# Windowed attention followed by a mixture of adapters: v cast by GpSimd's DMA queue and turned in one piece, q kept in natural order, and four smaller edits

## The chip, the cores and the metric

The kernel runs on one core of a Trainium2 chip. The metric is the device time of one execution in microseconds (us); three executions of the kernel before gave 203.4, 205.75 and 207.98 us, so the median is 205.75 us. The engines are called TensorE (PE in the profile, PEld for its weight loads), VectorE (DVE), ScalarE (ACT), GpSimd (POOL) and SyncE (SP, which only issues DMAs here).

## What is computed

```python
def _attn_ref(q, k, v):            # each (8, 8, 576, 64) float32
    scores = scale * np.matmul(q, k.transpose(0, 1, 3, 2))
    mask = np.abs(pos[:, None] - pos[None, :]) <= 32
    scores = np.where(mask, scores, -1000000000.0)
    ...
    return np.matmul(attn, v)

def _moe_ref(x, w_gate, A, B):     # x (4608, 512): the attention's output, heads side by side
    logits = x @ w_gate            # 8 experts, the best 2 are kept, softmax over these
    ...
            delta[mask] += w[mask, k, None] * (x[mask] @ A[e] @ B[e])
    return x + delta
```

There are 64 pairs of batch and head, each with 576 rows of 64. A row attends only to rows at most 32 away, so the scores are made in blocks: 64 keys against the 128 queries around them.

## The kernel before

**Tiles.** The 64 pairs are taken two at a time: one half of the partitions (64 of them) holds a pair of the first four batches, the other half one of the last four (`g` in the code). So there are 32 units of 9 blocks of 64 rows. The rows of all units, 32 x 576, are cut into 9 load tiles of 2,048 rows; the tiles are numbered t = 0 to 8. A tile's q and k are 1 MB of float32 each, and so is its v.

**q and k** (`load_qk`, L326 to L383). SyncE loads a tile with partitions of 16 rows each (`run_view`, L313); tile 0 comes in two pieces of 64 partitions. Two casts to float16 per tensor and tile (L350) run on GpSimd (for tile 0 partly on VectorE and ScalarE). TensorE turns each cast piece by eight matmuls with the identity (L359), and ScalarE or VectorE evicts the result from PSUM (L368) into `qT`, or into `kc` for k. GpSimd then spreads `kc` into `kT` (L379), a tile whose off-diagonal quarters were zeroed at the start, so that one 128-row weight holds both halves' keys. In `qT` and `kc` the 16 rows of a partition lie 128 columns apart.

**v** (`load_v`, L385 to L408). SyncE issues four DMAs of 32 partitions each per tile (L392; 2 KB runs in `half_view`), GpSimd casts the tile in one instruction (L397), and VectorE turns it straight into `vt` by two stream transposes of 32x32 blocks, one for each 64 partitions (L406). `vraw` has two buffers and `v16` one.

**Scores** (`score`, 36 groups of 8 blocks). Two matmuls put the mask into PSUM (L460), then each block's matmul adds the scores (L465); its queries are read from `qT` with 16 rows apart and its output is written to PSUM in the same strided order (`p[:, i].rearrange("m (p r) -> m r p", r=16)`). ScalarE's exp evicts a group into `PT` (L472).

**The rest.** `pv` multiplies by v (L500), and VectorE normalises (L510, L523) into `xs`. `moe` runs once for each quarter s of the units (for the last quarter in three parts): turn x (L550), evict (L560), logits and A (L587), gating by some twelve small VectorE instructions (L598 to L634), turn z (L643, L650), multiply by B (L663). VectorE then adds x while it evicts (L678) into one of four `ob` buffers, and SyncE stores from there (L688).

**What sets the order.** Every piece is an `Op` with the engines that may do it, a duration, the buffers that it holds and a due number (`prio`). `Plan.order` puts all pieces in one list by these estimates before anything runs, choosing an engine and a buffer for each; each engine then runs its share strictly in that order. A piece that holds a buffer waits until those who held it before are done; SyncE's DMA issues stand in the same kind of order, loads and stores in one queue. PSUM has three 1,024-column float32 tiles (`W`) for scores, PV, logits and adapter output, and two float16 tiles (`T`) for transposes.

Of the kernel before, what the change touches and what calls it, by code (L numbers as in the profile page):

```python
# [45 lines left out]
class Op:  # L46
    def __init__(self, eng, fn, bufs, need, make, prio, dma):
        self.eng, self.fn = eng, fn
        self.bufs, self.need, self.make = bufs, need, make
        self.prio, self.dma = prio, dma  # L50
        self.takes = len(eng) > 1 or fn.__code__.co_varnames[:1] == ("eng",)
        self.on = self.start = self.end = self.ready = None


class Plan:
    COST = {"DVE": 0.6}
# [25 lines left out]
    def order(self, slack):  # L82
# [23 lines left out]
        while left:  # L106
            can = []
            low = 1e9
            for o in left:
# [14 lines left out]
                for e, dur in o.eng.items():  # L124
# [3 lines left out]
                    ends.append((t + dur + self.COST.get(e, 0.0), t, e))  # L128
# [35 lines left out]
def kernel(  # L164
# [14 lines left out]
    POOLS = {"W": 3, "T": 2, "raw": 4, "vraw": 2, "c16": 5, "v16": 1,  # L179
# [5 lines left out]
    def many(name, shape, dt, pool=sb):  # L185
# [90 lines left out]
    for i, t in enumerate(phys["PT"]):
        fh = P.first_hold("PT", i)
        zeros(t[:, :, 0:64], fh, -90 + 5 * i)
        zeros(t[:, :, 192:256], fh, -90 + 5 * i)
    for i, t in enumerate(phys["vt"]):  # L280
        fh = P.first_hold("vt", i)
        zeros(t[0:64, :, D:], fh, -88 + 30 * i)
        zeros(t[64:128, :, 0:VD2], fh, -88 + 30 * i)
# [5 lines left out]
        op("DVE", 0.3, ones, bufs=[fh], need=[f"vz{i}"], prio=-88 + 30 * i)  # L289
# [33 lines left out]
    def load_qk(w, t):  # L323
        pieces = [(0, 64), (64, 64)] if t == 0 else [(0, 128)]
        raw = buf("raw", f"raw{w}{t}")
        src = run_view(w)  # L326
        dst = buf({"q": "qT", "k": "kc"}[w], f"{w}T{t}")
        if w == "q":
            qT[t] = dst
        else:  # L330
            kT[t] = buf("kT", f"kT{t}")
        due = 32 * t
        lp = -80 + due + (0 if w == "q" else 1)
        for pi, (p0, pn) in enumerate(pieces):
            op("SP", 0.4, lambda p0=p0, pn=pn: nc.sync.dma_start(  # L335
                out=ap(raw)[p0:p0 + pn], in_=src[128 * t + p0:128 * t + p0 + pn]),
                bufs=[raw], make=[(w, t, p0, "raw")], prio=lp + 0.5 * pi, dma=DMA_MB * pn / 128)
            for hf in range(2):
# [4 lines left out]

                def cast(eng=eng, p0=p0, pn=pn, hf=hf, c16=c16):
                    o = ap(c16)[p0:p0 + pn].rearrange("p r (g d) -> p r g d", g=2)
                    i = ap(raw)[p0:p0 + pn].rearrange("p g (f r d) -> p f r g d", f=2, d=D)[:, hf]
# [4 lines left out]
                dur = {"POOL": pool, "ACT": act, "DVE": dve32}[eng](1024)  # L351
                op(eng, dur, cast, bufs=[raw, c16], need=[(w, t, p0, "raw")],
                   make=[(w, t, p0, hf, "16")], prio=due - 30 + (0 if w == "q" else 1) + 0.1 * hf + .5 * pi)
                tp = buf("T", f"tp{w}{t}_{p0}_{hf}")

# [385 lines left out]
```

## Time and profile before

| | |
|---|---|
| median of 3 runs | 205.75 us |
| the profiled execution's own time | 205.5 us |
| its span, first to last instruction | 203.6 us |
| mean granted TensorE clock | 0.914 of 2.4 GHz |
| read from and written to memory | 28.85 MB and 9.44 MB |

The profile is one execution. Busy times of engines overlap; a group of instructions has the line, the engine, the operation, output<-input, and shapes as partitions x elements. "Idle before, <-releaser" is the time for which the engine waited just before the group and what ended the wait. DMA issues are listed under SP (SPq), the engine whose queue they stand in, and are not counted as busy.

### The profile page before, as it was taken

Reading aid. Unit: us, or ns where it says so; the run is one execution under the profiler, and the core shown is the slowest. Engines: PE = TensorE matmul, PEld = TensorE weight load, DVE = VectorE, ACT = ScalarE, POOL = GpSimd, SP = SyncE. Lnnn points to the kernel's source line nnn. Section 1 sums busy time; section 2 is a strip of 40 time slices with the busy share of each in tenths; the row PEclk is TensorE's granted clock in tenths of the full one; section 3 lists DMA queues with packets and bytes.
Section 4 is the critical chain, followed back from the end, with each engine's and each line's share of the span. In section 5 each row is a group of like instructions: output and inputs, shape, how many; then the busy total and the mean of one; then the engine's idle time right before and its main releaser. Section 6 shows DMA issues by size and latency. Waiting matters only on the chain.

```text
span 203.6 us, 3782 instructions
## 1 busy us (share of the span) xinstructions
PE 137.2 (67%) x1512; PEld 112.6 (55%) x1512; DVE 136.1 (67%) x230; ACT 92.5 (45%) x110; POOL 76.9 (38%) x80
## 2 busy tenths in 40 slices
PE   0250797949798919729329997659799958777450
PEld 0140586848697918418218897547589944665200
DVE  4641609729778797734046799978798487869652
ACT  8990149533586506700702864508447425143300
POOL 5345882568486458078233654720400000000000
PEclk9999999999999966985966999979999999999955
DMA  5999999999999999999559980001920002912252
GB/s 130 222 216 342 288 340 226 268 373 196 301 248 239 291 226 274 220 284 256 189 182 307 367 174 0 3 0 36 337 94 0 3 2 72 335 60 84 99 206 77
DMA packets 16705, 38.53 MB, mean 189 GB/s; under 512 B 2736, under 2 KB 2736, under 8 KB 16688
## 3 DMA queue, kind: packets, MB, share of 16 engines
q1 hardware_dynamic: 16688, 38.30, 67.5%
q8 instruction: 12, 0.20, 0.4%
q14 instruction: 5, 0.04, 0.1%
HBM read 28.85 MB, written 9.44 MB: 188 GB/s over the span
## 4 chain that ended last, share of the span: by engine, by line
DMA 45%; PE 27%; DVE 15%; issue 3%; POOL 3%; ACT 2%; SPq 2%; DVEq 0%; POOLq 0%; ACTq 0%
DMA vraw<-in_v_dram 28%; DMA raw<-in_k_dram 11%; PE W L465 8%; DMA out_dram<-ob 6%; DVE ob L678 5%; PE W L500 5%; PE W L460 4%; PE T L550 3%; PE W L587 3%; PE W L663 3%; DVE xs L523 2%; DVE vt L406 2%; DVE zs L634 2%; PE T L643 1%; SPq L335 1%
## 5 line engine op out<-in xcount | busy, mean ns | idle before, releaser
L472 ACT ACTIVATE PT<-W 128x1024 f16<-128x1024 f32 x36 | 36.8, 1024 | 65.0 <-PE W L465 59.2
L465 PEld LDWEIGHTS <-kT 128*128 128x128 f16 x304 | 35.2, 135 | 28.9 <-issue 20.6
L350 POOL CAST c<-raw 128x1024 f16<-128x1024 f32 (+1 forms) x37 | 37.6, 1038 | 31.6 <-DMA raw<-in_q_dram 18.0
L465 PE MATMUL W<-qT,kT 128*128 128x128 f16 (+3 forms) x304 | 47.5, 319 | 0.9 <-POOL kT L379 0.9
L359 PE MATMUL T<-ident,c 128*128 128x128 f16 (+1 forms) x320 | 23.7, 227 | 31.6 <-POOL c L350 20.7
L406 DVE STREAM_TRANSPOSE vt<-v 64x1024 f32<-64x1024 f32 x18 | 37.6, 2088 | 9.9 <-POOL v L397 9.7
L460 PE MATMUL W<-mask,perm 128*128 128x512 f16 x72 | 32.7, 454 | 15.5 <-DVE ob L678 7.5
L359 PEld LDWEIGHTS <-c 128*128 128x128 f16 (+1 forms) x320 | 19.9, 106 | 35.2 <-POOL c L350 21.7
L500 PE MATMUL W<-vt,PT 128*128 128x130 f16 x416 | 31.2, 228 | 3.3 <-ACT PT L472 1.7
L678 DVE TENSOR_TENSOR ob<-W,xs 128x1024 f32<-128x1024 f32 (+1 forms) x23 | 23.9, 1078 | 14.0 <-DMA out_dram<-ob 9.1
L500 PEld LDWEIGHTS <-PT 128*128 128x128 f16 x416 | 27.7, 103 | 6.4 <-issue 5.2
L523 DVE TENSOR_TENSOR xs<-W,rc 128x640 f16<-128x640 f32 (+1 forms) x34 | 26.7, 785 | 1.4 <-PE T L550 0.2
L379 POOL COPY kT<-kc 64x1024 f32<-64x1024 f32 (+1 forms) x20 | 19.8, 990 | 19.0 <-ACT kc L368 17.9
L397 POOL CAST v<-vraw 128x2048 f16<-128x2048 f32 x9 | 17.0, 1894 | 17.3 <-DVE vt L406 6.7
L368 ACT COPY kc<-T 128x1024 f16<-128x1024 f16 (+1 forms) x16 | 14.3, 908 | 11.2 <-POOL kT L379 6.0
L368 ACT COPY qT<-T 128x1024 f16<-128x1024 f16 (+1 forms) x14 | 13.6, 979 | 10.1 <-PE T L359 9.1
L510 DVE RECIPROCAL rc<-W 128x10 f32<-128x10 f32 (+1 forms) x34 | 7.1, 210 | 14.4 <-PE W L500 14.2
L663 PE MATMUL W<-Bw,zT 128*128 128x512 f16 x40 | 13.4, 417 | 3.4 <-ACT zT L650 1.4
L560 ACT COPY xT<-T 128x1024 f16<-128x1024 f16 x12 | 11.9, 1010 | 4.9 <-PE T L550 4.8
L550 PE MATMUL T<-ident,xs 128*128 128x128 f16 x160 | 11.7, 221 | 0.9 <-DVE xs L523 0.9
L587 PE MATMUL W<-WA,xT 128*128 128x136 f16 x160 | 10.6, 223 | 1.6 <-ACT xT L560 1.2
L550 PEld LDWEIGHTS <-xs 128*128 128x128 f16 x160 | 10.6, 116 | 1.5 <-DVE xs L523 1.0
(49 smaller groups left out, 99.0 us busy)
## 6 DMA issues: line engine op xcount, KB each, us to landing
vraw<-in_v_dram SPq DMA_DIRECT2D x36, 256.0 KB, 13.1
raw<-in_q_dram SPq DMA_DIRECT2D x8, 1024.0 KB, 17.7
raw<-in_k_dram SPq DMA_DIRECT2D x8, 1024.0 KB, 20.2
out_dram<-ob SPq DMA_DIRECT2D x24, 256.0 KB, 3.4
out_dram<-ob SPq DMA_DIRECT2D x16, 192.0 KB, 3.1
raw<-in_q_dram SPq DMA_DIRECT2D x2, 512.0 KB, 5.7
raw<-in_k_dram SPq DMA_DIRECT2D x2, 512.0 KB, 9.2
ob<-in_moe_A_dram SPq DMA_DIRECT2D x1, 256.0 KB, 11.6
```

What stands on the lines that cost most here:

```text
L350: (nc.vector if eng == "DVE" else nc.gpsimd).tensor_copy(out=o, in_=i)
L359: nc.tensor.matmul(out=o[:, r], lhsT=ap(c16)[p0:p0 + pn, r], rhs=ident[p0:p0 + pn, p0:p0 + pn], is_transpose=True, start=True, stop=True)
L368: (nc.vector.tensor_copy if eng == "DVE" else nc.scalar.copy)(out=o, in_=i)
L379: (nc.vector if eng == "DVE" else nc.gpsimd).tensor_copy(out=o, in_=i)
L406: nc.vector.transpose(out=o, in_=i)
L460: nc.tensor.matmul(out=p[:, 4 * j:4 * j + 4], lhsT=perm, rhs=bcast(mask, 1, 4), start=True, stop=False)
L465: nc.tensor.matmul(out=o[:, :, c0:c0 + w], lhsT=ap(kT[t])[:, s], rhs=ap(qT[tq])[:, :, c:c + w], start=False, stop=(n == len(mine) - 1))
L472: op("ACT", act(1024), lambda: nc.scalar.activation(out=ap(pt)[:, :, 64:192], in_=ap(ps).rearrange("m (i c) -> m i c", c=128), func=AF.Exp ...
L500: nc.tensor.matmul(out=ap(po)[:, GS * j:GS * j + 2 * VD2 - 2], lhsT=ap(PT[ti])[:, pos, off:off + 128], rhs=ap(vt[t])[:, sl, :], start=st, ...
L523: nc.vector.tensor_tensor(out=o, in0=i, in1=bcast(ap(rc)[:, 0:n], 3, D), op=ALU.mult)
L550: nc.tensor.matmul(out=ap(tp)[:, 512 * i + 128 * c:512 * i + 128 * c + 128], lhsT=ap(xs[s])[:, b, g].rearrange("p (m c) -> p c m", c=4)[:, c],
L678: nc.vector.tensor_tensor(out=ap(ob)[:, 0:m], in0=ap(pd)[:, 0:512 * m].rearrange("p (i c) -> p i c", c=512), in1=i1, op=ALU.add)
```

## The change

- `load_v`: v is loaded by DMAs that GpSimd issues, which cast to float16 on the way (`v16`, two buffers; `vraw` is gone). A partition now reads one run of 8 KB (`half_view` with r=32). One stream transpose over 128 partitions (L412) writes a new tile `vc`, and two copies of 64 partitions (L422) spread it into `vt`; GpSimd does these (for tile 0 VectorE, ScalarE or GpSimd).
- q stays in natural order: the eviction of the turned q (L378) writes `qT` with rows in their own order and reads PSUM with the stride instead; the scores' matmul (L480) reads and writes without strides.
- k: `kT` takes its 64 keys in another order, by the spread (L391) and by the permutation `perm` of the mask.
- Tile 0 of q and k is loaded by halves of each partition's rows over 128 partitions, and VectorE does its four casts.
- From quarter 2 on, `BY_PE` picks adapter outputs (2 of the 6 in quarter 2 and all 5 in quarter 3) for which TensorE adds x by a matmul with the identity (L690), so that ScalarE can evict by a plain copy (L698).
- The zeroing at the start is spread over later due numbers, and the planner's estimates (`COST`, `pool`, `dve_sb`) change.

```diff
-    COST = {"DVE": 0.6}
+    COST = {"DVE": 0.8, "ACT": 0.4}
...
-    POOLS = {"W": 3, "T": 2, "raw": 4, "vraw": 2, "c16": 5, "v16": 1,
+    POOLS = {"W": 3, "T": 2, "raw": 4, "c16": 5, "v16": 2, "vc": 2,
...
-        return qrows[w].rearrange("(g b) h (s i f r) d -> (b h s) i f g (r d)", g=2, i=4, f=2, r=8)
+        return qrows[w].rearrange("(g b) h (s f r) d -> (b h s) f g (r d)", g=2, f=2, r=32)
...
+        if t == 0:
             for hf in range(2):
+                op("SP", 0.62, lambda hf=hf: nc.sync.dma_start(
+                    out=ap(raw)[:, :, 512 * hf:512 * hf + 512],
+                    in_=src[:, :, 512 * hf:512 * hf + 512]),
+                    bufs=[raw], make=[(w, t, "raw", hf)], prio=-200 + 2 * hf + late, dma=DMA_MB / 2)
...
+            op({"DVE": dve_sb(1024)} if t == 0 else {"POOL": pool(1024)}, 0,
+               cast, bufs=[raw, c16],
+               need=[(w, t, "raw", hf)], make=[(w, t, hf, "16")], prio=due - 30 + late + 0.1 * hf)
...
-                    o = ap(dst)[:, 8 * hf:8 * hf + 8, p0:p0 + pn]
-                    i = ap(tp)[:, 0:8 * pn].rearrange("m (r p) -> m r p", r=8)
+                if w == "q":
+                    o = ap(dst).rearrange("m (p f r) -> m f p r", f=2, r=8)[:, hf]
+                    i = ap(tp).rearrange("m (r p) -> m p r", r=8)
...
+                    o = ap(kT[t])[m0:m0 + 64, :, m0:m0 + 64].bitcast(F32).rearrange(
+                        "m s (f r) -> m s f r", f=2)
+                    i = ap(dst)[m0:m0 + 64].bitcast(F32).rearrange("m r (s f) -> m s f r", f=2)
...
-                op("SP", 0.4, lambda p0=p0, f=f, g=g: nc.sync.dma_start(
-                    out=ap(raw)[p0:p0 + 32].rearrange("p (i x) -> p i x", i=4),
-                    in_=src[32 * t:32 * t + 32, :, f, g]),
-                    bufs=[raw], make=[("v", t, "raw")], prio=-78 + due + .1 * p0 / 64,
-                    dma=DMA_MB / 4)
-        op("POOL", pool(2048), lambda: nc.gpsimd.tensor_copy(out=ap(v16), in_=ap(raw)),
-           bufs=[raw, v16], need=[("v", t, "raw")], make=[("v", t, "16")], prio=due - 14)
+                op("POOL", 0.6, lambda p0=p0, f=f, g=g: nc.gpsimd.dma_start(
+                    out=ap(v16)[p0:p0 + 32], in_=src[32 * t:32 * t + 32, f, g]),
+                    bufs=[v16], need=[("k", 0, "raw", 0)] if t == 0 else [],
+                    make=[("v", t, "16")], prio=-60 + due + .1 * p0 / 64, dma=DMA_MB / 4 * 1.15)
+
+        def turn():
+            i = ap(v16).bitcast(F32).rearrange("p (i r w) -> p w r i", i=2, w=32)
+            o = ap(vc).bitcast(F32).rearrange("p s w -> p w s").rearrange(
+                "p w (a b) -> p w a b", b=2)
+            nc.vector.transpose(out=o, in_=i)
+        op("DVE", 2.1, turn, bufs=[v16, vc], need=[("v", t, "16")], make=[("vc", t)], prio=due - 10)
         for g in range(2):
-            def turn(g=g):
...
-                nc.vector.transpose(out=o, in_=i)
...
+            def spread(eng, g=g):
                 m0 = 64 * g
+                o = ap(dst)[m0:m0 + 64, :, VD2 * g:VD2 * g + D].bitcast(F32)
+                i = ap(vc)[m0:m0 + 64].bitcast(F32)
...
-                    o = p[:, i].rearrange("m (p r) -> m r p", r=16)
-                    nc.tensor.matmul(out=o[:, :, c0:c0 + w], lhsT=ap(kT[t])[:, s],
-                                     rhs=ap(qT[tq])[:, :, c:c + w],
+                    nc.tensor.matmul(out=p[:, i, c0:c0 + w], lhsT=ap(kT[t])[:, s],
+                                     rhs=ap(qT[tq])[:, c:c + w],
...
+                        nc.tensor.matmul(out=o, lhsT=ap(zT)[:, j + i], rhs=Bw,
+                                         start=True, stop=not by_pe)
+                        if by_pe:
+                            nc.tensor.matmul(out=o, lhsT=ident, rhs=x_of()[:, i],
+                                             start=False, stop=True)
...
+                    if by_pe:
+                        nc.scalar.copy(out=ap(ob)[:, 0:m], in_=i0)
...
+def BY_PE(s, w, j):
+
+    return s >= 2 and (s == 3 or j == 2)
```

On GpSimd, one load tile in the middle of the program takes these rows before (`v_72` is `v16`, `c_` the cast q and k; the rows belong to neighbouring tiles because each is due at another time):

```order
L397 CAST v_72<-vraw_65 128x2048
L379 COPY kT_78<-kc_79 64x32x32 x2
L350 CAST c_67<-raw_63 128x1024
L350 CAST c_69<-raw_63 128x1024
L350 CAST c_70<-raw_64 128x1024
L350 CAST c_68<-raw_64 128x1024
```

and these in the changed kernel:

```order
L403 DMA v_70<-in_v_dram 32x2048 x4
L391 COPY kT_79<-kc_80 64x32x32 x2
L357 CAST c_67<-raw_63 128x1024
L357 CAST c_68<-raw_63 128x1024
L422 COPY vt_84<-vc_72 64x32x32 x2
L357 CAST c_69<-raw_64 128x1024
L357 CAST c_65<-raw_64 128x1024
```

The long cast of v has left GpSimd's queue; the four DMA issues and two copies into `vt` have come to stand between the casts and spreads of q and k.

On VectorE, the start of the program (tile 0, before the first score) reads before:

```order
L264 MEMSET PT_87 128x8x32
L350 CAST c_67<-raw_61 64x1024
L350 CAST c_69<-raw_61 64x1024
L264 MEMSET kT_78 64x32x32
L287 MEMSET vt_82 64x32
L288 MEMSET vt_82 64x32
L264 MEMSET vt_83 64x32x33
L368 COPY qT_73<-T_108 128x8x64
```

and now:

```order
L357 CAST c_65<-raw_61 128x1024
L268 MEMSET vt_83 64x32x33
L357 CAST c_66<-raw_62 128x1024
L357 CAST c_67<-raw_61 128x1024
L378 COPY kc_80<-T_110 128x1024
L357 CAST c_68<-raw_62 128x1024
L291 MEMSET vt_83 64x32
L292 MEMSET vt_83 64x32
L268 MEMSET kT_79 64x32x32 x2
L391 COPY kT_77<-kc_80 64x32x32
```

All four casts of tile 0 and one of the two spreads of its k have come to VectorE, with two zeroings of a later `kT` ahead of the spread.

On ScalarE, the last evictions of the scores and what follows read in the changed kernel (`ob` is the output buffer, `W` the PSUM tile; before, ScalarE wrote no `ob`):

```order
L487 ACTIVATE PT_88<-W_108 128x8x128
L698 COPY ob_99<-W_106 128x1024
L575 COPY xT_92<-T_110 128x1024
L698 COPY ob_98<-W_106 128x1024
L487 ACTIVATE PT_89<-W_108 128x8x128
L487 ACTIVATE PT_85<-W_107 128x8x128
```

Seven such copies in all take the place of seven of VectorE's seventeen 1,024-column additions.

## Rows read from the trace of the kernel before

**Rows 1.** Stages: length, busy PE, PEld, DVE, ACT, POOL, PEclk, DMA share, GB/s.

```profile
0.00:25.15 25.15, 7.28 (x75) 5.43 (x76) 12.01 (x21) 14.97 (x23) 13.42 (x26) 1.00 0.93 240
25.15:92.40 67.25, 50.76 (x586) 43.35 (x585) 45.89 (x62) 34.29 (x38) 39.80 (x36) 0.93 1.05 269
25.15:179.60 154.45, 119.04 (x1335) 100.73 (x1334) 109.02 (x165) 71.62 (x78) 63.44 (x56) 0.92 0.70 195
179.60:203.70 24.10, 10.87 (x107) 6.46 (x104) 15.12 (x44) 5.91 (x10) 0.00 (x0) 0.77 0.28 100
```

**Rows 2.** Timeline of the start: start us, length us, instruction [idle before <-releaser].

```profile
6.40 1.22 DVE L350 CAST c<-raw 64x1024 f16<-64x1024 f32 x2
12.92 1.04 POOL L350 CAST c<-raw 64x1024 f16<-64x1024 f32 x1 [1.32 <-DMA raw<-in_k_dram]
22.79 0.98 PE L465 MATMUL W<-qT,kT 128*128 128x96 f16 x4 [0.87 <-POOL kT L379]
25.15 1.02 ACT L472 ACTIVATE PT<-W 128x1024 f16<-128x1024 f32 x1 [3.10 <-PE W L465]
```

**Rows 3.** The chain that ended last, in order of time: start, length, what.

```profile
69.94 22.42 DMA raw<-in_k_dram
92.38 11.96 DMA out_dram<-ob
```

**Rows 4.** The same chain by line, shares of the span.

```profile
DMA vraw<-in_v_dram 28%; DMA raw<-in_k_dram 11%; PE W L465 8%; DMA out_dram<-ob 6%; DVE ob L678 5%; PE W L500 5%; PE W L460 4%; PE T L550 3%; PE W L587 3%; PE W L663 3%; DVE xs L523 2%; DVE vt L406 2%; DVE zs L634 2%; PE T L643 1%; SPq L335 1%
```

**Rows 5.** Groups of instructions by shape: busy us, mean ns, idle before.

```profile
L406 DVE STREAM_TRANSPOSE vt<-v 64x1024 f32<-64x1024 f32 x18 | 37.6, 2088 | 9.9 <-POOL v L397 9.7
L350 POOL CAST c<-raw 128x1024 f16<-128x1024 f32 x32 | 32.4, 1038 | 25.6 <-DMA raw<-in_q_dram 13.8 <-DMA raw<-in_k_dram 8.4 <-PE T L359 3.0
L678 DVE TENSOR_TENSOR ob<-W,xs 128x1024 f32<-128x1024 f32 x17 | 20.1, 1218 | 13.7 <-DMA out_dram<-ob 9.1 <-PE W L663 4.2
L379 POOL COPY kT<-kc 64x1024 f32<-64x1024 f32 x16 | 17.3, 1082 | 18.1 <-ACT kc L368 17.2 <-DVE kc L368 0.5
L397 POOL CAST v<-vraw 128x2048 f16<-128x2048 f32 x9 | 17.0, 1894 | 17.3 <-DVE vt L406 6.7 <-DMA vraw<-in_v_dram 3.8 <-DVE sm L601 3.0
L368 ACT COPY qT<-T 128x1024 f16<-128x1024 f16 x13 | 13.0, 1009 | 10.1 <-PE T L359 9.1 <-DVE sm L599 1.0
```

**Rows 6.** Short stretches of the load phase, columns as in rows 1.

```profile
5.00:10.00 5.00, 1.21 (x16) 0.90 (x17) 3.36 (x7) 4.94 (x10) 1.90 (x2) 1.00 1.02 219
15.00:20.00 5.00, 0.00 (x0) 0.00 (x0) 0.35 (x1) 0.48 (x1) 2.21 (x2) 1.00 1.05 331
40.00:45.00 5.00, 2.36 (x32) 1.95 (x30) 1.36 (x3) 2.03 (x3) 2.68 (x3) 1.00 1.01 370
45.00:50.00 5.00, 4.76 (x67) 4.23 (x65) 4.11 (x5) 2.19 (x3) 4.39 (x5) 1.00 1.08 200
```

**Rows 7.** The chain again, two pieces of TensorE where it never waits.

```profile
117.80 0.44 PE W L465 x4
...
123.94 0.75 PE W L500 x13
```

**Rows 8.** Waits of ScalarE's exp: us in total, times, longest us.

```profile
ACT PT L472 <- PE W L465: 59.2, 29, 10.8
```

**Rows 9.** The issues of v's DMAs (line 392): ns min/median/max, first and last start us.

```profile
L392 SPq DMA_DIRECT2D vraw<-in_v_dram x36: 560/566/653, 3.5 to 113.7; - x36
```

**Rows 10.** GpSimd's timeline at the end of its casts.

```profile
125.20 3.01 POOL L350 CAST c<-raw 128x1024 f16<-128x1024 f32 x3 [2.99 <-PE T L359]
129.49 1.90 POOL L397 CAST v<-vraw 128x2048 f16<-128x2048 f32 x1 [1.27 <-issue]
```

**Rows 11.** The exps (line 472) after that: ACT busy (count), PEclk, DMA share, GB/s.

```profile
128.20:203.70 75.50, 13.31 (x13) 0.90 0.27 95
```

**Rows 12.** VectorE's timeline, one small instruction beside a GpSimd cast and one alone.

```profile
129.55 1.86 DVE L620 TENSOR_SCALAR sm<-sm 128x10 f32<-128x10 f32 x1
...
164.06 0.17 DVE L620 TENSOR_SCALAR sm<-sm 128x10 f32<-128x10 f32 x1
```

More of the change, by code (lines that the diff above doesn't have):

```diff
@@ L288, in ones @@
             nc.vector.memset(t[64:128, :, D + 1:D + 2], 1.0)
-        op("DVE", 0.3, ones, bufs=[fh], need=[f"vz{i}"], prio=-88 + 30 * i)
+        op("DVE", 0.3, ones, bufs=[fh], need=[f"vz{i}"], prio=-155 if i == 0 else 32 * i - 40)
     wb = P.first_hold("ob", 0)
@@ L350, in cast @@
                         (nc.vector if eng == "DVE" else nc.gpsimd).tensor_copy(out=o, in_=i)
[L351 to L354, printed above, removed]
-                def trans(p0=p0, pn=pn, hf=hf, c16=c16, tp=tp):
-                    o = ap(tp)[:, 0:8 * pn].rearrange("m (r p) -> m r p", r=8)
-                    for r in range(8):
-                        nc.tensor.matmul(out=o[:, r], lhsT=ap(c16)[p0:p0 + pn, r],
-                                         rhs=ident[p0:p0 + pn, p0:p0 + pn], is_transpose=True,
-                                         start=True, stop=True)
@@ L407, in load_v @@
-            op("DVE", 0.15 + 1.067, turn, bufs=[v16, dst], need=[("v", t, "16")],
-               make=[("vt", t)], prio=due - 10)
+                o = ap(dst)[m0:m0 + 64, :, VD2 * g:VD2 * g + D].bitcast(F32)
+                i = ap(vc)[m0:m0 + 64].bitcast(F32)
+                if eng == "ACT":
+                    nc.scalar.copy(out=o, in_=i)
+                else:
+                    (nc.vector if eng == "DVE" else nc.gpsimd).tensor_copy(out=o, in_=i)
+            op({"POOL": 0.99, "DVE": dve_sb(1024), "ACT": act(1024)} if t < 1 else {"POOL": 0.99}, 0, spread, bufs=[vc, dst],
+               need=[("vc", t)], make=[("vt", t)], prio=due - 8)
@@ L433, in run_deps @@
             t, c = divmod(NB * 64 * u + row, 2048)
-            r.add((kind, t, 64 * (c // 1024) if t == 0 else 0))
+            r.add((kind, t))
         return r
@@ L444, in score @@
             t, s = slot(u, a)
-            need |= {("kD", t, 64 * (s // 16) if t == 0 else 0)}
+            need |= {("kD", t)}
             bufs.add(kT[t])
@@ L659, in moe, with x_of @@
                 dt = (s, pair[0])
-                def delta(j=j, m=m, pd=pd, zT=zT):
-                    for i in range(m):
-                        nc.tensor.matmul(out=ap(pd)[:, 512 * i:512 * i + 512],
-                                         lhsT=ap(zT)[:, j + i], rhs=Bw, start=True, stop=True)
-                op("PE", m * mm(512), delta, bufs=[pd, zT], need=[("zT", tok, w), "Bw"],
-                   make=[("pd", dt)], prio=pq)
-                def add(pair=pair, pd=pd, ob=ob, m=m):
+                def x_of(pair=pair, m=m):
                     x = ap(xs[s]).rearrange("p b g c -> p (b g) c")
```

143 lines of the change are left out of this document (74 added, 69 removed).

## The prediction

> **What bounds the kernel now.** I read the busy times by stage first [rows 1]. Two moments cut the span of 203.6 us: the first exp of a score group at 25.15 us [rows 2] and the last at 179.6 us. The reader is to see that no engine is full: in the 154.5 us between them TensorE is busy 119.0 us (77%), VectorE 109.0 (71%), GpSimd 63.4 (41%). Up to 92.4 us the 16 DMA engines are full (share 1.05) at 269 GB/s; over the whole of the stage the share is only 0.70. So the first half waits for loads, and the second half works off a backlog on TensorE and VectorE.
>
> Second, the chain that ended last, in order of time [rows 3]: up to 92.4 us it is made of loads, among them one of k that took 22.42 us to land behind what stood ahead of it in the queue; then a store that landed after 11.96 us, for which VectorE's output addition waited 9.1 us [rows 5]. That is a hole between the halves. By line, loads of v and k are 39% of the span on this chain [rows 4].
>
> Third, the rate in short stretches [rows 6]. At 5 to 10 us, when pieces of 64 partitions move, 219 GB/s; at 45 to 50 us, with v's 32-partition pieces, 200; at 15 to 20 and 40 to 45 us, with q and k in 128 partitions, 331 and 370. All at a share above 1. The narrow pieces, not the bytes, use up the DMA engines.
>
> Fourth, TensorE where it never waits [rows 7]: four score matmuls take 0.44 us, 0.110 each, while thirteen of PV, hardly wider (130 columns), take 0.75, or 0.058 each. Both load a new 128x128 weight each time; what differs is the stride of the scores' input and output.
>
> The sum is made against the profiled execution's own 205.5 us (the span and 1.9 around it), 0.25 us under the median of 205.75. A difference under 2% (4 us) can hardly be told from none here.
>
> **The change part by part.**
>
> *Start.* Before, the four pieces of tile 0's q and k are cast from 6.40 to 12.92 us [rows 2], a step of 2.2 us each, as 0.5 MB at 219 GB/s gives (2.4). In 128 partitions at 350 GB/s (between 331 and 370) a piece takes 1.5 us: they land at about 5.5, 7.0, 8.5 and 10.0. Behind the last come a VectorE cast (0.65, near the 0.61 each of the two in the row at 6.40), eight turns (0.6, taken as eight PV matmuls with some start-up), an eviction (1.0), the spread (1.1, as GpSimd's now; two zeroings ahead of it on VectorE run while TensorE and ScalarE work) and the first scores (2.4, from 22.79 to 25.15). That makes 15.7 instead of 25.15, also because v's GpSimd cast no longer stands among k's. If the pieces kept their old step, 18.6. So -6.6 to -9.5; I take -9, since both rates are this kernel's own rows.
>
> *Work between the first and the last exp.* Scores: 304 matmuls become cheaper by up to 0.110 - 0.058 = 0.052 us, 15.8 us of TensorE; four added matmuls of 512 columns give back 0.9 (0.058 x 512/130 = 0.23 each). TensorE goes from 119.0 to 104. VectorE: 16 of the 18 transposes lie here, at 2.088 us [rows 5]; the free size stays 1,024 words and the partitions double, so 8 go, -16.7; two output additions go to ScalarE, -2.4; some evictions come, +1. It goes from 109.0 to 91. ScalarE gets two copies of some 1.0 us and q's eviction with a strided read: between its 1,009 ns now and twice that (as VectorE's strided transpose takes 2,088 ns for 1,024 words), up to 16 us more. It waited 59.2 us for scores [rows 8], so I cost this at nothing; without that cover it would be 16.
>
> TensorE stays the busiest. At the same share of 77% its 104 us need 135 instead of 154.5: -19.5, the upper bound. The lower bound is what lies on the chain [rows 4]: scores for 8% of the span, 16 us, of which half goes, and transposes for 2%, 4 us, of which at most all go: -12. I take -16, in the middle, since the saving falls on both engines that feed each other.
>
> What is late next? DMAs: a tile's q and k take 2.1 MB/350 = 6.0 us; its v 1.05 MB between 3.0 (at 350) and 5.2 us (at 200, the row of 32-partition pieces): 9.0 to 11.2 a tile, 81 to 101 us for nine. That is under 135. GpSimd is the nearer limit. A tile costs it four casts (4 x 1.038), two spreads of k (2 x 1.082), two of v (the same shape, the same 1.082) and four DMA issues: 8.5 us + 4x. The trace of before shows no issue by GpSimd. Bounds for x: 0.57 us, SyncE's for the same DMAs [rows 9], and 1.9, GpSimd's longest row. I take 1.0, an ordinary GpSimd instruction: 12.5 us a tile. From 8 us on (its first issues wait for k's first piece), eight further tiles put the last cast at about 108 us instead of 128.2 [rows 10]. What follows took 75.5 us with 13 of the 36 score groups [rows 11] and becomes about 66 (13 x 8 x 0.052 = 5, two transposes 4). With the 1.9 around the span that gives 176. So GpSimd and TensorE agree, and every 0.1 us of x beyond is worth 3.2 us.
>
> The Trainium skill, "GPSIMD Engine Reference", section 7 on pitfalls for Q7 kernels, speaks against the spread of k: reads with a step above 8 bytes cost about 2.9 cycles an element instead of 1.9. The new spread reads 256 bytes apart, and no GpSimd row of before has such a step, so the trace can't confirm it. By that rule the 1.082 would be some 1.6 us (an estimate from the page's ratio), a tile 13.6 and the end 9 us later.
>
> *The added wait.* A v issue now stands in GpSimd's own queue and waits until its `v16` buffer has been turned. Queued behind it are the next tile's spreads and casts; TensorE's turns wait for these, and the scores for those. Before, that wait stood in SyncE's queue. VectorE's transposes come early enough as long as v lands on time; I cost that, with small VectorE instructions that GpSimd's longer use holds up (1.86 us beside a cast [rows 10] against 0.17 alone [rows 12]), at +3, between 0 and +9 (five such pairs of stalls).
>
> *Hole.* Stores still share SyncE's queue with q and k, but v's pieces are gone from it and the loads need less time. Between 0 and the 9.1 us waited; I take -5.
>
> *Tail.* From the last exp to the end 24.1 us, VectorE busy 15.1 [rows 1]. Five additions (5 x 1.218) leave it; each that lies on the chain becomes two added matmuls (0.46 at full clock, 0.9 at half; the stage's mean is 0.77) and a ScalarE copy of 1.0, up to 0.7 more than it was. Between +1.5 and -4; I take -2.
>
> *Sum.* -9 - 16 + 3 - 5 - 2 = -29: 205.5 - 29 = 176.5 us. All good ends: -9.5 - 19.5 - 9.1 - 4 = -42, 163. All bad ends of the forecast's own terms: -6.6 - 12 + 9 + 1.5 = -8, 197.
>
> **Rivals.**
>
> *Gains beside the path.* The scores' matmul is paced by its weight loads and not by strides, and the hole stays, because q and k loads stand ahead of the stores as before. Then only start, transposes, tail and the added wait count: -9 - 4 - 2 + 3 = -12, 193 us. For it: ScalarE, TensorE and VectorE wait for each other in short turns, so work taken off one need not show. Against: PV loads a new weight as often and takes 0.058.
>
> *GpSimd is full.* With x at 1.9 a tile takes 16.1 us and the same sum as above gives 8 + 129 + 66 + 1.9 = 205: a wash. Then the change does not do what it says, since v's cast only turns into issues. For it: GpSimd's strict order and the wait above. Against: it was busy 41%, and 17 us of casts go.
>
> *Slower.* The same place, but each issue is held up: at x = 2.5 a tile takes 18.5 us and the end is 224. It decides from x = 2.05 on (16.7 a tile, 209.5 us). Nothing in the trace of before shows GpSimd issuing DMAs; what it shows is that VectorE and GpSimd hold each other up [rows 10, 12].
>
> The Trainium skill, "SBUF — State Buffer", in its box on VectorE blocking software DMAs, says that a VectorE copy in its fast two-port mode keeps GpSimd from writing descriptors, so that a DMA of some 620 ns took about 3,100; by that rule the end would lie in this rival. Against it: by the order only tile 0 has copies from SBUF to SBUF on VectorE, later ones read PSUM. No run here shows it yet.
>
> **How the numbers follow.** Forecast 0.62, gains beside the path 0.20, GpSimd full 0.09, slower 0.09. The first two are faster by over 2% (under 201.6 us): 0.82. GpSimd full is within 2%: 0.09. Slower: 0.09. The range, 164 to 204, holds the forecast, the first rival and half of the second.
>
> **What would show it.** Right: the first exp at 15 to 17 us; score matmuls at some 0.055 us each in a chain without waits; nine transposes of about 2.1 us; GpSimd's last cast near 108 us; stretches of the load phase with q, k and v together above 300 GB/s; no wait of VectorE for a store near 9 us. Wrong: four issues on GpSimd that take over 6 us of a tile; TensorE's turns waiting for casts all through; v landing later than q and k of the same tile; ScalarE without idle time, from q's evictions.

## The result and the profile after

The changed kernel takes 171.08 us (median of 4 executions, 170.41 to 174.94) against 205.23 (203.4 to 207.98) for the kernel before on the same chip: a ratio of 0.836, 95% interval 0.829 to 0.844. The forecast was 176.5 us, in a range from 164 to 204. Some executions of most kernels are over 1.5% longer than its fastest, the profiled one of the changed kernel among them (174.94 us at a mean granted clock of 0.905; the three timed ones ran at 0.94), so a difference below is between the medians of all four, and a number in brackets right behind it is the same difference between the faster executions alone.

The columns are those of [rows 1], the stages others: up to the first exp, to the end of GpSimd's last cast of q and k, to the end of the last exp, to the end. The second of these stages in the kernel before stands first:

```profile
25.15:128.20 103.05, 78.00 (x880) 67.17 (x879) 67.80 (x94) 49.94 (x55) 57.34 (x51) 0.90 0.92 246
```

```profile
0.00:16.34 16.34, 5.93 (x43) 4.29 (x44) 11.91 (x22) 13.81 (x18) 8.71 (x24) 1.00 0.88 259
16.34:113.73 97.39, 75.04 (x962) 62.74 (x961) 66.34 (x98) 55.81 (x62) 82.73 (x86) 0.89 0.77 230
113.73:151.00 37.27, 32.28 (x396) 24.91 (x394) 28.62 (x58) 20.06 (x23) 12.10 (x8) 0.95 0.36 122
151.00:173.20 22.20, 12.56 (x98) 6.98 (x97) 10.13 (x40) 8.49 (x12) 0.00 (x0) 0.80 0.32 117
```

The reader is to see that the second stage has another full engine than before: GpSimd, 82.7 of 97.4 us (85%) instead of 57.3 of 103.1 (56%), while the DMA share fell from 0.92 to 0.77. In the third TensorE is the full one (32.3 of 37.3, 87%).

The chain that ended last, by engine and by line, says the same. Loads of k and v, 39% of it before [rows 4], are gone, and GpSimd's spread of k leads. The 10% of DMA is one load, that of A: it landed at 21.8 us, and on ScalarE its cast stands ahead of the next eviction of q.

```profile
PE 34%; POOL 21%; DVE 17%; DMA 10%; ACT 7%; issue 6%; SPq 2%; DVEq 0%; POOLq 0%; ACTq 0%
POOL kT L391 12%; DMA ob<-in_moe_A_dram 10%; PE W L480 6%; PE W L476 6%; PE W L515 5%; PE W L687 5%; DVE vc L412 3%; POOL c L357 3%; PE W L602 3%; POOL vt L422 3%; POOL v L403 3%; PE T L565 3%; PE T L365 2%; PE W L690 2%; ACT PT L487 2%
```

Groups by shape, as in [rows 5] (busy us, mean ns, idle before):

```profile
L357 POOL CAST c<-raw 128x1024 f16<-128x1024 f32 x32 | 32.3, 1044 | 11.7 <-DMA raw<-in_q_dram 6.9 <-DMA raw<-in_k_dram 2.5 <-PE T L365 1.8
...
L391 POOL COPY kT<-kc 64x1024 f32<-64x1024 f32 x16 | 31.8, 1989 | 3.3 <-ACT kc L378 2.8
...
L403 POOL DMA_DIRECT2D v<-in_v_dram x36 | 19.0, 539 | 0.0
...
L412 DVE STREAM_TRANSPOSE vc<-v 128x1024 f32<-128x1024 f32 x9 | 18.5, 2061 | 0.5 <-issue 0.4
...
L422 POOL COPY vt<-vc 64x1024 f32<-64x1024 f32 x17 | 17.9, 1056 | 7.4 <-DVE rc L525 4.1 <-DVE vc L412 2.8
...
L378 ACT COPY qT<-T 128x1024 f16<-128x1024 f16 x16 | 16.1, 1012 | 2.6 <-PE T L365 2.5
...
L700 DVE TENSOR_TENSOR ob<-W,xs 128x512 f32<-128x512 f32 x6 | 4.1, 682 | 0.6 <-DMA out_dram<-ob 0.6
```

Two prices differ from the prediction's: the issue of a v DMA takes 0.54 us on the mean and the spread of k 1.99 (1.08 before). Nine transposes cost 2.06 us each, ScalarE's eviction of q kept its price, and VectorE waits 0.6 us for stores instead of 9.1.

Waits of ScalarE's exp (33.3 us, against 59.2 in [rows 8]), GpSimd's queue at its first and its last casts of tiles 1 to 8, and two chains of scores:

```profile
ACT PT L487 <- PE W L480: 33.3, 22, 5.9
```

```profile
16.64 2.02 POOL L357 CAST c<-raw 128x1024 f16<-128x1024 f32 x2 [6.89 <-DMA raw<-in_q_dram]
...
109.67 4.06 POOL L357 CAST c<-raw 128x1024 f16<-128x1024 f32 x4
113.67 4.00 POOL L391 COPY kT<-kc 64x1024 f32<-64x1024 f32 x2
```

```profile
31.33 0.43 PE W L480 x4
...
126.16 0.22 PE W L480 x4
```

At 126 us four scores take 0.22 us, 0.055 each, half of [rows 7]. At 31 us they take twice that: there the clock was granted mostly at the lower of its two levels, 1.2 GHz (0.55 of 2.4 on the mean), after five microseconds in which TensorE worked 0.67 us and GpSimd 4.75 (stretches of 5 us, columns as above):

```profile
25.00:30.00 5.00, 0.67 (x7) 0.51 (x7) 2.63 (x2) 1.97 (x3) 4.75 (x3) 0.77 1.02 414
30.00:35.00 5.00, 5.00 (x42) 4.09 (x41) 0.90 (x2) 2.05 (x2) 4.96 (x8) 0.55 0.92 228
```

### The profile page after: what moved, and what is told of

Same layout as the page of the kernel before. It is cut to its first block, busy times and chain, and to the rows that moved or that the text cites. A ratio compares the mean times of both kernels' runs of the same rounds, so it can differ in the third digit from the quotient of the medians.

```text
span 173.2 us, 3742 instructions
## 1 busy us (share of the span) xinstructions
PE 125.8 (73%) x1494; PEld 98.9 (57%) x1494; DVE 117.0 (68%) x218; ACT 98.2 (57%) x113; POOL 103.5 (60%) x117
## 3 DMA queue, kind: packets, MB, share of 16 engines
q0 software_dynamic: 1728, 4.72, 14.9%
## 4 chain that ended last, share of the span: by engine, by line
PE 34%; POOL 21%; DVE 17%; DMA 10%; ACT 7%; issue 6%; SPq 2%; DVEq 0%; POOLq 0%; ACTq 0%
POOL kT L391 12%; DMA ob<-in_moe_A_dram 10%; PE W L480 6%; PE W L476 6%; PE W L515 5%; PE W L687 5%; DVE vc L412 3%; POOL c L357 3%; PE W L602 3%; POOL vt L422 3%; POOL v L403 3%; PE T L565 3%; PE T L365 2%; PE W L690 2%; ACT PT L487 2%
## 5 line engine op out<-in xcount | busy, mean ns | idle before, releaser
L487 ACT ACTIVATE PT<-W 128x1024 f16<-128x1024 f32 x36 | 36.5, 1025 | 37.0 <-PE W L480 33.3
L480 PEld LDWEIGHTS <-kT 128*128 128x128 f16 x304 | 24.5, 107 | 28.6 <-issue 9.9
L357 POOL CAST c<-raw 128x1024 f16<-128x1024 f32 x32 | 32.3, 1044 | 11.7 <-DMA raw<-in_q_dram 6.9
L480 PE MATMUL W<-qT,kT 128*128 128x128 f16 (+3 forms) x304 | 30.6, 231 | 10.7 <-POOL kT L391 8.1
L391 POOL COPY kT<-kc 64x1024 f32<-64x1024 f32 x16 | 31.8, 1989 | 3.3 <-ACT kc L378 2.8
L365 PE MATMUL T<-ident,c 128*128 128x128 f16 x288 | 24.5, 240 | 12.0 <-DVE c L357 7.8
L365 PEld LDWEIGHTS <-c 128*128 128x128 f16 x288 | 20.0, 108 | 15.3 <-DVE c L357 8.5
L422 POOL COPY vt<-vc 64x1024 f32<-64x1024 f32 x17 | 17.9, 1056 | 7.4 <-DVE rc L525 4.1
L403 POOL DMA_DIRECT2D v<-in_v_dram x36 | 19.0, 539 | 0.0
L412 DVE STREAM_TRANSPOSE vc<-v 128x1024 f32<-128x1024 f32 x9 | 18.5, 2061 | 0.5 <-issue 0.4
L378 ACT COPY qT<-T 128x1024 f16<-128x1024 f16 x16 | 16.1, 1012 | 2.6 <-PE T L365 2.5
L525 DVE RECIPROCAL rc<-W 128x10 f32<-128x10 f32 (+1 forms) x34 | 7.1, 209 | 13.6 <-PE W L515 13.6
L378 ACT COPY kc<-T 128x1024 f16<-128x1024 f16 x12 | 12.1, 1014 | 2.2 <-PE T L365 2.2
```

Source lines behind the costliest of these rows:

```text
L357: (nc.vector if eng == "DVE" else nc.gpsimd).tensor_copy(out=o, in_=i)
L365: nc.tensor.matmul(out=ap(tp)[:, 128 * r:128 * r + 128], lhsT=ap(c16)[:, r], rhs=ident, is_transpose=True, start=True, stop=True)
L378: (nc.vector.tensor_copy if eng == "DVE" else nc.scalar.copy)(out=o, in_=i)
L391: (nc.vector if eng == "DVE" else nc.gpsimd).tensor_copy(out=o, in_=i)
L403: op("POOL", 0.6, lambda p0=p0, f=f, g=g: nc.gpsimd.dma_start(out=ap(v16)[p0:p0 + 32], in_=src[32 * t:32 * t + 32, f, g]), bufs=[v16], nee ...
L412: nc.vector.transpose(out=o, in_=i)
```

## The experiments

Two theories at first: GpSimd's queue sets the pace of the new kernel (A), or TensorE does (B). After four runs a third: each in its own stretch (C). All medians are of four executions, those of before beside them of four to seven. The runs were made on several chips, on which the kernel before took 202.9 to 205.2 us (medians). The marks of every profile side by side, with the median of the executions (us):

| kernel | first exp | last cast of q, k ends | last exp ends | span | median |
|---|---|---|---|---|---|
| before | 25.2 | 128.2 | 180.6 | 203.6 | 205.2 |
| after | 16.3 | 113.7 | 150.9 | 173.2 | 171.1 |
| q strided again | 17.7 | 112.6 | 161.9 | 181.7 | 186.1 |
| v as before | 16.3 | 111.4 | 151.3 | 173.8 | 183.5 |
| x added by VectorE | 16.3 | 111.7 | 151.8 | 175.0 | 176.8 |
| spread in order | 15.7 | 102.6 | 143.3 | 165.5 | 164.8 |
| before with natural q | 24.6 | 124.5 | 173.9 | 197.0 | 197.1 |
| tile 0 in 64 partitions | 23.2 | 116.2 | 154.5 | 177.1 | 175.1 |
| k evicted straight | 14.9 | 97.2 | 137.6 | 159.3 | 163.4 |
| v spread twice | 16.3 | 121.1 | 160.2 | 182.5 | 185.4 |
| q strided, spread in order | 16.6 | 105.9 | 151.9 | 173.3 | 172.5 |
| after, second time | 16.8 | 113.3 | 150.2 | 172.4 | 173.3 |
| x added by VectorE, second time | 16.3 | 113.7 | 152.4 | 175.4 | 175.8 |

**q strided again.** The eviction and the scores' matmul are those of before:

```diff
...
-                    nc.tensor.matmul(out=p[:, i, c0:c0 + w], lhsT=ap(kT[t])[:, s],
-                                     rhs=ap(qT[tq])[:, c:c + w],
+                    o = p[:, i].rearrange("m (p r) -> m r p", r=16)
+                    qs = ap(qT[tq]).rearrange("m (r p) -> m r p", r=16)
+                    nc.tensor.matmul(out=o[:, :, c0 // 16:(c0 + w) // 16], lhsT=ap(kT[t])[:, s],
+                                     rhs=qs[:, :, c // 16:(c + w) // 16],
```

> The changed kernel with q laid out with the stride again (order of work unchanged). A score matmul should take 0.11 us again in a chain without waits, 304 x 0.055 = 16.7 us more of TensorE. Theory A (GpSimd paces the kernel until its last spread of k near 124 us, TensorE and VectorE only behind it): only the 13 to 15 score groups behind that count, +5 to +9 us over 171, so 176 to 180. Theory B (TensorE paces it throughout): +14 to +17, so 185 to 188.

Measured: 186.07 us (183.47 to 187.14), 15.0 (13.6) more than the changed kernel, in B's range and not in A's; ratio to before 0.921 (0.894 to 0.947). The widest of the scores' shapes in its profile, and the same three stages:

```profile
L482 PE MATMUL W<-qT,kT 128*128 128x128 f16 x210 | 38.6, 323 | 0.0
```

```profile
17.67:112.61 94.94, 75.97 (x924) 66.01 (x923) 62.41 (x93) 54.94 (x61) 82.37 (x86) 0.96 0.78 233
112.61:161.90 49.29, 41.34 (x430) 33.48 (x430) 34.20 (x64) 21.25 (x24) 11.86 (x8) 0.90 0.28 96
161.90:181.70 19.80, 10.29 (x100) 6.37 (x97) 10.13 (x40) 8.47 (x13) 0.00 (x0) 1.00 0.34 123
```

The dearer scores leave GpSimd's last cast where it was (112.6 against 113.7 us): up to there TensorE has room. Of B this leaves only the size. The loss lies behind that cast, 49.3 us instead of 37.3, where TensorE is the full engine and has more left to do (430 matmuls instead of 396); the tail is 2.4 us shorter in this profile, and the spans differ by 8.5.

**v as before.** The four SyncE loads, GpSimd's cast and two transposes a tile; the spread of k reads two neighbouring words at a time again, each pair 256 bytes from the last.

```diff
-                op("POOL", 0.6, lambda p0=p0, f=f, g=g: nc.gpsimd.dma_start(
+                op("SP", 0.4, lambda p0=p0, f=f, g=g: nc.sync.dma_start(
...
+        op("POOL", pool(2048), lambda: nc.gpsimd.tensor_copy(out=ap(v16), in_=ap(raw)),
```

> The changed kernel with v's whole path as before (SyncE loads, GpSimd cast, two transposes of 64 partitions on VectorE) and with it the old key order in the spread of k; the planner makes a new order. Theory A with loads that fill the DMA engines again: 185 to 195 us, spread of k back at 1.08 us each. Theory B (v's path is beside TensorE's): 171 to 176.

Measured: 183.5 us; the three timed executions 183.2 to 185.4, the profiled one 175.8. The median is in neither theory's range, the profiled execution in B's. So v's new path is worth 12 us by the medians (4.7), and 0.8 when the two profiled executions are compared, both at a granted clock of 0.905; what it is worth stays open. Its chain, by engine and line:

```profile
DMA 45%; PE 28%; DVE 15%; issue 3%; SPq 2%; ACT 2%; POOL 1%; DVEq 0%; POOLq 0%; ACTq 0%
DMA vraw<-in_v_dram 22%; DMA raw<-in_k_dram 17%; DMA out_dram<-ob 7%; PE W L507 5%; DVE vt L414 5%; PE W L594 4%; PE W L468 4%; PE W L679 3%; PE W L472 3%; PE T L557 3%; DVE ob L692 3%; PE W L682 2%; DVE xs L530 2%; PE T L650 1%; DVE zs L641 1%
```

Loads of v and k and the store are back on the chain, GpSimd is off it (1%). So the new v path exchanges a bound by loads (DMA share 1.00 from the first exp to the last cast of q and k) for one by GpSimd's queue. That the second ends earlier this profile doesn't show: the last cast ends at 111.4 us here and at 113.7 in the changed kernel.

**x added by VectorE**, twice, the second time beside the changed kernel itself:

```diff
-    return s >= 2 and (s == 3 or j == 2)
+    return False
```

> The changed kernel with every addition of x on VectorE. The prediction's tail term: +2 to +4 us over 171, so 173 to 175. Rival: the added matmuls and copies cost as much as VectorE's additions did, 170 to 172.

> The changed kernel itself, once more, beside the next run on the same chip, so that the two can be read against each other at like granted clocks. From the first measurement: 170 to 172 us.

> The changed kernel with x added by VectorE everywhere, once more. Theory of the prediction (the seven copies on ScalarE take 2 us from the end, most of it in the tail): 173 to 174 us beside 171 of the changed kernel, the tail from the last exp on 1 to 2 us longer. Rival (the first comparison, 176.8 against 171.1, holds: the added matmuls also spare VectorE before the last exp, where its seven additions stand between TensorE's pieces): 176 to 177 us, and the last exp itself 2 to 4 us later.

Measured: 176.76 (176.22 to 177.09) against 171.08, in neither range, then 175.76 (175.52 to 177.2) against 173.29 (171.3 to 175.0): the edit is worth 5.7 (5.7) and 2.5 (3.9) us. The second time falls between the two theories, and the changed kernel came out 1.3 us above what was expected of it. From the last exp's start to the end the first pair's profiles take 173.2 - 149.9 = 23.3 and 175.0 - 150.7 = 24.3 us, the second pair's 172.4 - 149.15 = 23.25 and 175.4 - 151.42 = 23.98. So 0.7 to 1.0 us of it lies in the tail, and the last exp itself comes 0.8 us later in the first pair and 2.3 in the second, as the rival said of the latter. The prediction's step that put the gain into the tail is borne out in part only.

**Spread of k in order.** GpSimd reads the same 1,024 words, but one after another (the keys then lie in another order than the mask's, so the values differ; the work doesn't):

```diff
-                    i = ap(dst)[m0:m0 + 64].bitcast(F32).rearrange("m r (s f) -> m s f r", f=2)
+                    i = ap(dst)[m0:m0 + 64].bitcast(F32).rearrange("m r w -> m (r w)").rearrange(
+                        "m (s f r) -> m s f r", f=2, r=16)
```

> The changed kernel whose spread of k reads its source in memory order, so the keys of a block are mixed up among kT's columns; same instructions in the same order, GpSimd's spread 1.06 to 1.1 us instead of 1.99, some 14.5 us less of GpSimd. Theory A: the last cast of q and k near 102 us instead of 114 and the end at 158 to 165 us. Theory B (TensorE paces it): 169 to 172.

Measured: 164.8 us (163.9 to 167.28), at the upper edge of A's range, with the last cast where A had it; ratio to before 0.820 (0.809 to 0.832).

```profile
L392 POOL COPY kT<-kc 64x1024 f32<-64x1024 f32 x16 | 17.0, 1062 | 6.1 <-ACT kc L378 5.7
```

The step of the read costs 1.99 - 1.06 = 0.93 us a copy, 14.8 us of GpSimd. Twelve of the sixteen copies stand ahead of the last cast, 11.1 us, and it comes 11.1 us earlier; the end comes 6.3 (6.9) earlier.

**Before with natural q.** The kernel before with that one edit.

```diff
-                    o = p[:, i].rearrange("m (p r) -> m r p", r=16)
-                    nc.tensor.matmul(out=o[:, :, c0:c0 + w], lhsT=ap(kT[t])[:, s],
-                                     rhs=ap(qT[tq])[:, :, c:c + w],
+                    nc.tensor.matmul(out=p[:, i, 16 * c0:16 * (c0 + w)], lhsT=ap(kT[t])[:, s],
+                                     rhs=ap(qT[tq])[:, 16 * c:16 * (c + w)],
```

> The kernel before with one edit: q is evicted into natural order and the scores' matmul reads and writes without strides; v's path, the start, the spread and the tail are those of before. Theory C (both TensorE and GpSimd set the pace of the changed kernel, while loads set that of the first half of the kernel before): four score matmuls in a chain take 0.22 us, TensorE's busy time falls by some 16 us, but up to 92 us the loads still decide, so only the scores behind that show: 13 of the 36 groups after the last cast, 13 x 8 x 0.055 = 5.7 us, and some more: -6 to -9 us, 196 to 199. Theory B (TensorE's time is on the path everywhere): -14 to -17 us, 187 to 191. Theory A (hidden anyway): within 3 us of before.

Measured: 197.14 us (188.96 to 198.78) beside 202.91 (196.83 to 205.97), a difference of 5.8 (8.3) between medians that both scatter by more; no ratio with an interval came of it. In size it is about C's, and 0.4 (0.6) of the 15.0 (13.6) us that the same edit is worth in the changed kernel.

**Tile 0 in pieces of 64 partitions.**

```diff
-                    out=ap(raw)[:, :, 512 * hf:512 * hf + 512],
-                    in_=src[:, :, 512 * hf:512 * hf + 512]),
+                    out=ap(raw)[64 * hf:64 * hf + 64],
+                    in_=src[64 * hf:64 * hf + 64]),
```

> The changed kernel, but tile 0's q and k come in two pieces of 64 partitions each, as before, instead of two row halves over 128 partitions; which engine does what, and in which order, is kept. Theory of the prediction (a late start is passed on to the end): each of the four pieces takes 2.2 us instead of 1.5, so the first exp comes 2 to 3 us later, at 18 to 19 us, and the end 2 to 3 us later, 173 to 174 us. Rival (GpSimd's casts and issues set the pace from 8 us on, so the end doesn't move as long as tile 1 lands at the same time): within 1 us of 171.

Measured: 175.1 us (174.73 to 178.9), above the range of the first theory and far from the rival's; ratio to before 0.885 (0.878 to 0.893). The first exp came at 23.2 us, 6.9 later and not 2 to 3, because each cast still takes half of the rows of all partitions and so waits for both pieces: the first cast starts at 11.19 us instead of 5.68. The end moved by 4.0 us (4.0). A late start is passed on, but only in part.

The run shows something else beside it. First the changed kernel's first eight v issues on GpSimd and one of VectorE's casts of tile 0, then the same two here, where the casts come after the issues:

```profile
4.33 5.42 POOL L403 DMA_DIRECT2D v<-in_v_dram  x8
7.54 0.69 DVE L357 CAST c<-raw 128x1024 f16<-128x1024 f32 x1
```

```profile
4.32 4.02 POOL L403 DMA_DIRECT2D v<-in_v_dram  x8
11.19 0.69 DVE L357 CAST c<-raw 128x1024 f16<-128x1024 f32 x1 [5.44 <-DMA raw<-in_q_dram]
```

In the changed kernel three of the eight issues overlap a cast; they took 0.73, 0.99 and 0.94 us, and each ended 0.10 us after its cast. Here the same three took 0.49 to 0.50.

**k evicted straight** from PSUM into its block-diagonal tile, in four pieces a tile, without the spread:

```diff
+                    def straight(eng, hf=hf, tp=tp, g=g):
+                        m0 = 64 * g
+                        o = ap(kT[t])[m0:m0 + 64, :, m0:m0 + 64].bitcast(F32).rearrange(
+                            "m s (f r) -> m s f r", f=2)[:, :, :, 8 * hf:8 * hf + 8]
+                        i = ap(tp)[m0:m0 + 64].bitcast(F32).rearrange(
+                            "m (r s f) -> m s f r", f=2, s=32)
+                        (nc.vector.tensor_copy if eng == "DVE" else nc.scalar.copy)(out=o, in_=i)
```

> The changed kernel, but the turned k goes from PSUM straight into its block-diagonal tile, in four pieces of 64 partitions and 512 words per tile done by ScalarE or VectorE; GpSimd's two spreads of k (1.99 us each) and the intermediate tile are gone. Theory C (GpSimd and TensorE set the pace together; work of GpSimd is worth about half at the end, as the run with the ordered spread showed): GpSimd loses 4 us a tile, 34 us in all, its last cast of q and k comes before 95 us, TensorE becomes the only bound, and the end is at 155 to 163 us. Rival D (evictions in four small pieces cost ScalarE and VectorE more than GpSimd gives: 0.5 us each become 1 us with their strided writes, and TensorE's turns wait for them): 165 to 172 us.

Measured: 163.42 us (161.33 to 164.82), ratio to before 0.823 (0.811 to 0.835), 7.7 us (7.7) less than the changed kernel: the lowest median of this case, 1.4 us under that of the spread in order, whose four executions overlap with its own. It misses C's 155 to 163 by a little, and its last cast ended at 97.2 us, not before 95.

```profile
L378 ACT COPY kT<-T 64x512 f32<-64x512 f32 x26 | 15.0, 579 | 5.2 <-DVE kT L378 4.2 <-PE T L364 0.5
```

```profile
14.88:97.17 82.29, 67.76 (x911) 56.48 (x910) 61.31 (x96) 53.55 (x67) 61.44 (x75) 0.94 0.90 276
```

```profile
PE 45%; DVE 27%; DMA 11%; ACT 6%; issue 5%; POOL 2%; SPq 1%; DVEq 0%; ACTq 0%; POOLq 0%
```

GpSimd is off the chain (2%); TensorE (45%) and VectorE (27%) lead it. The DMA share of the stretch up to the last cast is up to 0.90, but the chain's one load there is that of tile 1's k, which landed at 20.4 us. Why C's number was missed stays open.

**v spread twice.** From tile 1 on GpSimd writes each half of `vt` twice.

```diff
                     (nc.vector if eng == "DVE" else nc.gpsimd).tensor_copy(out=o, in_=i)
+                    if t >= 1:
+                        nc.gpsimd.tensor_copy(out=o, in_=i)
```

> The changed kernel, but from tile 1 on GpSimd does each of the two spreads of v twice (the second copy writes the same values again): 16 more copies of 1.06 us, 17 us of GpSimd, the order of everything else kept. Theory C in its sharper form (up to GpSimd's last cast of q and k, which ended at 113.7 us, GpSimd alone sets the pace; what is left behind it takes TensorE and VectorE some 57 us): the last cast ends at 126 to 130 us, the rest takes 52 to 57 us, since TensorE comes there with less left to do; the end is at 180 to 188 us. Rival (GpSimd is only one of several limits, as the half of the ordered spread's saving that reached the end would say): last cast at 119 to 123, end at 176 to 180 us. Rival (GpSimd's work is hidden): within 2 us of 171.

Measured: 185.39 us (184.2 to 187.57), 14.3 (13.3) more for 16.8 us of added GpSimd work. The last cast ended at 121.1 us, not at 126 to 130 but in the first rival's range: 12 of the added copies stand ahead of it, 12.6 us, of which 7.4 came through; in the changed kernel GpSimd had waited some 14.7 us in that stretch, which can take up the rest. GpSimd's last spread of v ends at 137.9 us instead of 126.9. The chain, by engine:

```profile
POOL 46%; PE 20%; DMA 14%; DVE 7%; issue 5%; ACT 3%; SPq 2%; POOLq 0%; DVEq 0%; ACTq 0%
```

So the end is where C put it and the last cast where the rival did; neither is borne out whole. On this chain GpSimd stands until its last spread of k, which ended at 133.5 us, behind the last cast; in the changed kernel it leaves the chain with the last casts, at 110.8.

**q strided and spread in order**, both edits together.

> The changed kernel with two earlier edits together: q strided again for the scores (alone: 186 us, last cast at 112.6 us) and the spread of k read in order (alone: 164.8 us, last cast at 102.6 us; keys are in another order than the mask's, so the output's values differ, the amount of work does not). Theory C in its sharper form (two phases in a row: GpSimd until its last cast, TensorE behind it): the last cast comes at 102 to 105 us as with the spread alone, the rest takes the 49 + 20 us that it took with q strided alone, and the end is at 172 to 177 us. Rival (TensorE's whole work is the bound once its scores are dear, so GpSimd's saving adds nothing): 183 to 187 us.

Measured: 172.51 us (170.54 to 175.08). The rival (TensorE's whole work is the bound) is excluded: with dear scores GpSimd's saving still brings 186.1 - 172.5 = 13.6 us (13.4) of its 14.8, more than the 6.3 (6.9) that it brings with cheap ones. This falls in C's range; why the saving shows more fully here the profiles don't settle, since the spans of the two differ by 8.4 us, not 13.6.

## Why the prediction was right, and by which steps

The forecast was -29 us. Between the two profiled executions the stages up to the first exp, up to the last exp's start and behind it give -8.8, -20.9 and -0.8, the span -30.4; the medians differ by 34.2. Taken back one at a time, natural q costs 15.0 us at the end, v's path 0.8 to 12, the additions on TensorE 2.5 to 5.7, and the start 4.0 (first exp at 23.2 us instead of 16.3); such losses need not add up, and the widest of them is v's.

**Start, -9: right.** VectorE's four casts of tile 0 began at 5.68, 7.54, 8.48 and 10.04 us, where the prediction had the pieces land at 5.5, 7.0, 8.5 and 10.0. The first exp came at 16.34 us (15.7 predicted), 14.9 to 17.7 in the profiles of kernels with tile 0 over 128 partitions. That it counts fully at the end is not borne out: 4.0 of 6.9 us.

**Work between the exps, with the added wait and the hole, -16 + 3 - 5 = -18: right.** From first to last exp 154.5 us became 149.9 - 16.3 = 133.6, -20.9; only the sum of the three terms is measured. TensorE was put at 104 us there and took 106.2, VectorE at 91 and took 94.5. The scores' price was right: 0.055 us where it runs freely. The rival *gains beside the path* fell: taking the strides back costs 15.0 us (13.6).

**GpSimd, 12.5 us a tile: right by luck, since two errors cancel.** By the rows after: 4 x 1.044 + 2 x 1.989 + 2 x 1.056 + 4 x 0.539 = 12.4. The term x was mis-sized (0.54 instead of 1.0, under its lower bound of 0.57), which took 1.84 off a tile, and the spread of k was mis-sized (1.99 instead of 1.08), which put 1.81 on. The second is the case of which the Trainium skill, "GPSIMD Engine Reference", section 7, warned. In direction the trace agrees; the price is higher than the 1.6 us estimated from its ratio: 1.87 times the copy in order. That no GpSimd row of before has such a step is true only of single words: its spread jumped 256 bytes after every pair of words and cost 1.08 [rows 5]. Had x been right at 1.0, the spread alone would have brought the last cast 12 x 0.91 = 11 us later, as the spread in order confirms from the other side (11.1).

**Last cast at 108 us: 113.7.** The casts of the eight tiles took 97.0 us, from 16.64 to 113.67, near the 100 put down, and this too is in part luck. GpSimd worked 82.7 us of that stretch, since four of the sixteen spreads of k come behind the last cast, and waited the other 14.7, for which this sum had nothing. They began at 16.6 and not at 8, because GpSimd waited 6.89 us for tile 1's q; the DMA engines were full meanwhile (share 1.06). What follows was put at 66 us with 13 score groups and took 59.5 with 11.

**Added wait, +3: not isolated.** GpSimd waits for nothing ahead of its v issues (0.0 in their group), so the wait that gave the term its name did not come; VectorE's blocked small instructions are there, as [rows 10, 12] let expect, but before had them too, and no run shows what more of them costs. On the chain, three beside GpSimd's work and two of them later, alone:

```profile
71.66 1.64 DVE sm L637
73.32 0.98 DVE sm L638
74.32 1.08 DVE sm L639
...
137.77 0.25 DVE sm L638
138.05 0.25 DVE sm L639
```

**Hole, -5: right in direction**, the wait for stores fell by 8.5 us (0.6 instead of 9.1); no run isolates what of it reaches the end. **Tail, -2: mis-sized.** In the profile the tail is 23.3 us instead of 24.1, -0.8; the edit is worth 2.5 to 5.7 us, of which the two pairs of profiles put 1.0 and 0.7 into the tail and 0.8 and 2.3 ahead of the last exp. Where the rest of it lies they don't show.

**Rivals on GpSimd.** *GpSimd is full* and *slower* named the right engine; x at 0.54 decided against them. Their slope, one us at the end for one of GpSimd, was a little high upward (14.3 of 16.8 us, v spread twice) and far too high downward (6.3 of 14.8, spread in order). So would an engine behave that is just the bound, with TensorE close behind: it costs nearly in full when it gets slower and gives less when it gets faster. This is argued and not shown, and the 13.6 of 14.8 with strided q don't fit it.

The Trainium skill's box on VectorE blocking software DMAs ("SBUF — State Buffer") came to pass in small, beside tile 0's casts alone: three issues that overlap them lasted until 0.10 us after the cast, up to 0.99 us and not the 3.1 of the prediction, and the first eight took 5.42 us instead of the 4.02 with the casts out of their way. It cost the end nothing that can be seen, since GpSimd waits 6.89 us for q right behind. From tile 2's on, where VectorE has no such casts, an issue takes 0.50 us, and a piece of v (256 KB as read) lands 6.0 us after it (median), against 7.3 and 9.5 for 1 MB of q and of k.

## What to carry to other kernels

Look for the engine that sets each stretch, not the span: here GpSimd up to about its last cast, TensorE behind it, and one edit (q in natural order) was worth 6 us (8) where loads were the bound and 15 (14) where they weren't. When work is moved into the queue of an engine that runs strictly in order, price each instruction with its access pattern; a copy that has to reorder is best done where it costs nothing, here in ScalarE's eviction from PSUM, and not one word at a time on GpSimd.

## What the runs showed of the hardware

- GpSimd's copy of 1,024 float32 words on 64 partitions took 1.06 us read in order, 1.08 read in pairs of words 256 bytes apart [rows 5] and 1.99 in single words 256 bytes apart. ScalarE's copy of the same shape from SBUF took 1.92 in single words (at 12.90 us, line 389) and 1.06 in pairs (with v as before, line 386).
- The same step in a read from PSUM (1,024 float16 words on 128 partitions, q written in runs of eight) cost ScalarE nothing: 1,012 ns for q with the step, 1,014 for `kc` without. VectorE took 1,224 instead of 687.

```profile
L378 ACT COPY kc<-T 128x1024 f16<-128x1024 f16 x12 | 12.1, 1014 | 2.2 <-PE T L365 2.2
...
L378 DVE COPY kc<-T 128x1024 f16<-128x1024 f16 x6 | 4.1, 687 | 3.8 <-PE T L365 3.8
...
L378 DVE COPY qT<-T 128x1024 f16<-128x1024 f16 x2 | 2.4, 1224 | 6.0 <-PE T L365 6.0
```

- GpSimd's issue of a casting DMA (32 partitions of 8 KB) took 0.50 us of its time from tile 2's on, somewhat less than SyncE's 566 ns for a plain one [rows 9], whether VectorE worked or not. Where it overlapped one of VectorE's casts from SBUF to SBUF it lasted until 0.10 us after the end of the cast, up to 0.99 us.
